# An order of issue written out for each engine, in place of a list scheduler with tables of offsets

## The chip, the cores and the metric

The kernel runs on one core of one Trainium2 chip. The metric is the device time of an execution in microseconds, as the median of several runs.

## The reference

Sequence S = 2048, model width D = 640, 32 heads of 20, hidden width F = 1728. All arrays are float32.

```python
def _A_ref(x, wqkv, wo):            # sliding, dilated attention
    W, dil = 8, 2
    q, k, v = split(x @ wqkv)       # 32 heads of 20
    idx = pos[:, None] - (jnp.arange(W) * dil)[None, :]
    logits = einsum("bhsd,bhswd->bhsw", q, k[idx]) * scale   # -1e9 where idx < 0
    o = einsum("bhsw,bhswd->bhsd", softmax(logits), v[idx])
    return o @ wo

def _B_ref(x, w1, b1, w2):          # dense, Mish, dense
    h = x @ w1 + b1
    return (h * jnp.tanh(softplus(h))) @ w2

x = A_x
g = sigmoid((x * gate_w).sum(-1, keepdims=True))
return g * _A_ref(x, wqkv, wo) + (1 - g) * _B_ref(x, w1, b1, w2)
```

## The kernel before

**The work.** Every float32 operand of a matmul is split into two halves: a "high" one that ScalarE (ACT) copies out of the loaded buffer, and a "low" one, the difference, which VectorE (DVE) or GpSimd (POOL) subtracts (`split`, L865 to L878: the ACT copy is L873, the subtraction L876). Each product is three matmuls on TensorE (PE): high x high, high x low, low x high (`mm3`, L932 to L934). A buffer of two halves is a `pair`, a landing buffer a `raw`, an `hb` or a `z`.

The stages, in the order of time: projections to q, k, v for eight units of work (two halves of the sequence by four groups of eight heads; `qkv`, with the first group written as passes at L1074); beside them the first dense layer in blocks, most of them as "quads" that need seven products in place of eight and use sums and differences of blocks (`quad`, `sum_into`, L1227); the attention of each unit on DVE in large operations of 128 x 2560 elements (L985 and L988 for the scores, L1023 and L1032 for the outputs); then the second dense layer (`mlp2`, matmul groups at L1687 and L1688), also with such sums; then the output projection (`wo_out`), with additions of PSUM banks to SBUF on DVE (L1919) and a gate multiplication (L1607). Attention outputs, activations and sums go through DRAM and come back. SyncE (SP) issues almost all DMAs; POOL issues the 52 that accumulate into DRAM (`plus`, L1170).

There are seven PSUM banks for matmuls. A projection's bank is emptied by small ACT copies (L1080, L1082, L1084, and L1086 for the gate's column in the first group of heads); a quad takes up to five banks.

**The order.** The program is written as 2668 tasks, numbered as they are made, each with an engine, a cost in ns, the tasks it waits for, and the buffers it takes and holds. 412 elementwise tasks are for "ANY" engine, which means DVE or POOL. `Plan.run` (L565) plays the tasks through in an event loop when the kernel is built, and issues each task's instructions at the moment its engine is idle and the task is ready. Among ready tasks it takes the least by rank and by due time on PE; both are shifted by five tables of offsets for single tasks (`MOVED`, `HELD_BACK`, `NEEDED`, `RANKED`, `ENGINE`, L81 to L525). A task for either engine goes to whichever asks for it first, within the rules of L619 to L631. On each engine, instructions run on the chip in the order in which they were issued, with semaphores between engines.

A large attention operation on DVE sets `quiet`, and a POOL task placed while it runs waits, by a semaphore, for the DVE instruction before it (`follow`, L656):

```python
                    if e == "POOL" and on and quiet > now and gate and ins:
                        self.follow(ins, gate)
```

The planner's costs: a DVE operation of n columns 75 + 1.03 n ns, times 1.025; a POOL operation 100 + 2.4 n; a large attention operation 2820, times 1.025; a DMA 450 to issue, its bytes at 330 B/ns on one wire, and 3000 more until it counts as landed.

Of the kernel before, what the change touches and what calls it, by code (L numbers as in the profile page):

```python
# [46 lines left out]
class Buf:  # L47
    def __init__(self, ring, make):
        self.ring, self.make, self.left, self.t, self.gone, self.can = ring, make, 0, None, None, None


class Ring:
    def __init__(self, n):
        self.free, self.line, self.at, self.left = n, [], 0, list(range(n))
# [12 lines left out]
class Task:  # L67
    def __init__(self, eng, ns, fn, rank, land):
        self.eng, self.ns, self.fn, self.rank, self.land = eng, ns, fn, rank, land
        self.waits, self.then, self.take, self.hold, self.both = 0, [], [], [], eng == "ANY"  # L70

def table(text):
    return {int(k): float(v) for k, v in (x.split(":") for x in text.split())}

MOVED = """2:-13 3:-34 5:27 6:38 7:-80 9:-9 10:16 12:-67 14:59 15:-7 17:-61 18:86 19:68 21:-84 22:-63 23:72 25:89 27:8 29:8  # L81
# [446 lines left out]
class Plan:  # L528


    NEAR, TURN, PATIENCE, HOP, STAY, HELD = 3564, 1936, 11000, 6531, 3456, 14750

    ORDERED = 1
    LAG = {"PE": 220, "ACT": 220, "DVE": 200, "POOL": 150, "SP": 3000}
# [30 lines left out]
    def run(self):  # L565
# [10 lines left out]
        for i, t in enumerate(self.tasks):  # L576
# [4 lines left out]
            if not t.waits:  # L581
                (shared if t.both else ready[t.eng]).append(t)
# [1502 lines left out]
```

## Time and profile before

| | |
|---|---|
| median of 3 runs | 617.6 us (616.7 to 618.37) |
| profiled execution | 616.73 us, its span 615.0 us |
| PE busy | 608.9 us (99%) |
| DVE busy | 577.1 us (94%) |
| ACT busy | 387.9 us (63%) |
| POOL busy | 311.2 us (51%) |

The span runs from the first to the last instruction of the profiled execution. Engines run side by side, so busy times do not add up. A matmul's end is modelled in the profile and lies beyond the start of the next one; the distance between starts tells its pace. In rows with a tile such as `pair<-raw`, the left name is written and the right ones are read; `side` and `bank` lie in PSUM, the others in SBUF. Behind `<-` in square brackets, or after "idle before", stands what ended the engine's idle time.

### The profile page before, as it was taken

The numbers are of one execution on the slowest core, as the hardware profiler recorded it, in microseconds if no ns is written. First come the engines' busy times: TensorE is split into PE (matmuls) and PEld (weight loads), VectorE is DVE, ScalarE is ACT, GpSimd is POOL, SyncE is SP. The second block draws the span as 40 slices with busy tenths as digits, with TensorE's granted clock in tenths as the row PEclk, the third lists the DMA queues.
The fourth block names the chain that finished last, engine by engine and source line by source line (L and its number), as shares of the span: only waits on it lengthen the run. The fifth ranks groups of instructions, "written<-read, shape, count | busy, mean of one in ns | idle before, by whom it ended". The sixth has DMA issues, their size and how long they took to land.

```text
span 615.0 us, 8940 instructions
## 1 busy us (share of the span) xinstructions
PE 608.9 (99%) x2693; PEld 504.7 (82%) x2693; DVE 577.1 (94%) x531; ACT 387.9 (63%) x854; POOL 311.2 (51%) x293
## 2 busy tenths in 40 slices
PE   8999999999999999999999999999999999999997
PEld 6888888888888888788888888888888888888885
DVE  4999999999998999999999999999999999999962
ACT  5746774768575767876666654583867574684721
POOL 2736566476283654654457657668554444601200
PEclk9999999999999999999999999999999999999999
DMA  8864679999999689999998999789999998996423
GB/s 301 254 192 149 178 220 305 280 252 305 257 268 300 172 240 273 261 242 259 291 267 219 286 289 290 243 245 299 332 377 352 283 386 276 321 354 197 147 89 119
DMA packets 106128, 159.43 MB, mean 259 GB/s; under 512 B 12112, under 2 KB 47952, under 8 KB 106048
## 3 DMA queue, kind: packets, MB, share of 16 engines
q1 hardware_dynamic: 98976, 146.01, 73.2%
q0 software_dynamic: 7104, 12.85, 13.7%
q8 instruction: 21, 0.34, 0.2%
q14 instruction: 27, 0.22, 0.1%
HBM read 91.90 MB, written 64.36 MB: 254 GB/s over the span
## 4 chain that ended last, share of the span: by engine, by line
PE 98%; DMA 1%; ACT 0%; SPq 0%; issue 0%; ACTq 0%
PE bank L932 32%; PE bank L934 32%; PE bank L933 32%; DMA z<-in_wq 1%; PE bank L1687 1%; PE bank L1688 1%; PE bank L1074 0%; SPq L882 0%; ACT pair L873 0%; ACT kvq L1801 0%; ACT kvq L1080 0%; ACT kvq L1082 0%; ACT hx L1084 0%; ACT zt L1086 0%; ACTq L1801 0%
## 5 line engine op out<-in xcount | busy, mean ns | idle before, releaser
L932 PE MATMUL bank<-pair,pair 128*128 128x512 f32 (+2 forms) x774 | 299.5, 387 | 0.4 <-ACT zt L1086 0.4
L933 PE MATMUL bank<-pair,pair 128*128 128x512 f32 (+2 forms) x774 | 299.7, 387 | 0.0
L934 PE MATMUL bank<-pair,pair 128*128 128x512 f32 (+2 forms) x774 | 299.7, 387 | 0.0
L932 PEld LDWEIGHTS bank<-pair,pair 128*128 128x128 f32 x774 | 145.4, 188 | 29.4 <-ACT zt L1086 0.8
L934 PEld LDWEIGHTS bank<-pair,pair 128*128 128x128 f32 x774 | 145.4, 188 | 28.7
L933 PEld LDWEIGHTS bank<-pair,pair 128*128 128x128 f32 x774 | 145.3, 188 | 28.7
L876 POOL TENSOR_TENSOR pair<-raw,pair 128x512 fp32r<-128x512 f32 (+3 forms) x82 | 104.8, 1303 | 86.9 <-ACT pair L873 30.2
L876 POOL TENSOR_TENSOR pair<-pair 128x512 fp32r<-128x512 f32 (+1 forms) x65 | 82.9, 1294 | 56.5 <-ACT pair L873 21.6
L873 ACT ACTIVATE pair<-pair 128x512 fp32r<-128x512 f32 (+1 forms) x139 | 79.6, 612 | 38.8 <-DMA pair<-act 18.7
L1023 DVE TENSOR_TENSOR pr<-kvq,side 128x2560 f32<-128x2560 f32 x32 | 90.3, 2822 | 1.1
L1032 DVE TENSOR_REDUCE kvq<-pr 128x320 f32<-128x2560 f32 x32 | 90.1, 2816 | 0.6
L988 DVE TENSOR_REDUCE lg<-pr 128x128 f32<-128x2560 f32 x32 | 90.0, 2812 | 0.6
L985 DVE TENSOR_TENSOR pr<-kvq,side 128x2560 f32<-128x2560 f32 x32 | 89.8, 2806 | 0.6 <-ACT lg L1000 0.5
L873 ACT ACTIVATE pair<-raw 128x512 fp32r<-128x512 f32 (+3 forms) x125 | 72.6, 613 | 18.5 <-PE bank L934 5.2
L1080 ACT ACTIVATE kvq<-bank 128x320 f32<-128x320 f32 x64 | 27.7, 434 | 49.1 <-PE bank L934 48.9
L876 DVE TENSOR_TENSOR pair<-pair 128x512 fp32r<-128x512 f32 (+1 forms) x74 | 46.7, 671 | 0.9 <-ACT pair L873 0.9
L932 PE MATMUL bank<-kvq,pair 128*128 128x512 f32 x102 | 40.0, 392 | 0.0
L933 PE MATMUL bank<-kvq,pair 128*128 128x512 f32 x102 | 39.8, 390 | 0.0
L934 PE MATMUL bank<-kvq,pair 128*128 128x512 f32 x102 | 39.8, 390 | 0.0
L1227 POOL TENSOR_TENSOR raw<-raw,raw 128x256 f32<-128x256 f32 (+1 forms) x25 | 24.4, 978 | 22.6 <-DVE side L1026 7.8
L876 DVE TENSOR_TENSOR pair<-raw,pair 128x512 fp32r<-128x512 f32 (+3 forms) x43 | 32.9, 785 | 1.7 <-ACT pair L873 1.7
L1374 ACT ACTIVATE bank<-bank 128x512 f32<-128x512 f32 x36 | 21.0, 584 | 13.7 <-PE bank L934 13.5
(119 smaller groups left out, 590.9 us busy)
## 6 DMA issues: line engine op xcount, KB each, us to landing
pair<-actt SPq DMA_DIRECT2D x54, 256.0 KB, 5.0
pair<-act SPq DMA_DIRECT2D x38, 256.0 KB, 4.8
raw<-in_w SPq DMA_DIRECT2D x34, 256.0 KB, 4.7
raw<-in_wq SPq DMA_DIRECT2D x30, 248.0 KB, 4.5
raw<-in_x SPq DMA_DIRECT2D x29, 256.0 KB, 5.1
actt<-hb SPq DMA_DIRECT2D x28, 256.0 KB, 3.6
actt<-z SPq DMA_DIRECT2D x24, 256.0 KB, 6.6
act<-z SPq DMA_DIRECT2D x24, 256.0 KB, 5.7
```

What stands on the lines that cost most here:

```text
L873: a = add("ACT", act_ns(n), lambda: A.activation(hi(), raw(), AF.Copy), after, rank=rank, take=take, hold=hold, kind="hi")
L876: return (V if e == "DVE" else G).tensor_tensor(lo(), raw(), hi().bitcast(F32), op=OP.subtract)
L932: nc.tensor.matmul(ps, ah, bh, start=first, stop=False, skip_group_check=more)
L933: nc.tensor.matmul(ps, ah, bl, start=False, stop=False, skip_group_check=more)
L934: nc.tensor.matmul(ps, al, bh, start=False, stop=last, skip_group_check=more)
L985: return V.tensor_tensor(pr, window(kv, s0, 0), qs[:, :, None, :].to_broadcast([128, 2, W, QF]), op=OP.mult)
L988: return V.tensor_reduce(lg_w[:, s0:s0 + 2], pr.rearrange("p s w (h d) -> p s w h d", d=DH), op=OP.add, axis=AX.X)
L1023: return V.tensor_tensor(twos, vw, pw[:, :, :, :, None, None].to_broadcast([128, 2, W, HQ, DH // 2, 2]), op=OP.mult)
L1032: return step("DVE", 2820, lambda: V.tensor_reduce(q[:, s0:s0 + 2].rearrange("p s (f j) -> p f s j", j=2), by_place, op=OP.add, axis=AX.X) ...
L1080: a = add("ACT", 330, lambda: A.activation(kv[:, 7 + s], ps.t[:, QF:3 * QF].rearrange("p (a b) -> p a b", a=2), AF.Copy), [done] + before, ...
L1227: return (V if e == "DVE" else G).tensor_tensor(t.t[:, i:i + n], a.t[:, j:j + n], b.t[:, k:k + n], op=op)
L1374: return add("ACT", 590, lambda: A.activation(to.t, of.t, AF.Copy), after, rank=-0.6, take=[to], hold=[of], kind=kind)
```

## The change

The five tables, the ranks, the due times and the event loop's choices are gone. In their place stands `ISSUE`, which lists for each of the five engines its tasks in the order of issue (and with that, for each "ANY" task, which engine does it), and `TAKEN`, which says for five rings of buffers which engine takes the next one. `Plan.run` walks the five lists: at each step it works out when the head of each list could start, and issues the earliest. Buffers go by the time at which they become free.

The planner's model of DVE and POOL differs. A DVE operation that reads two SBUF operands is marked `alone`; every "ANY" task is so marked. A POOL task from the "ANY" kind does not start while an `alone` operation runs on DVE, nor so that it would run into the next one, and an `alone` operation does not start while such a POOL task runs. Each such POOL task is tied by a semaphore to a DVE instruction: the one running when it is to start, or the one before that. The costs change: a large attention operation 2740 ns, no factor of 1.025 on DVE (nor 1.1 on ACT), a POOL operation 120 + 2.2 n.

The tasks themselves, what they compute, and the sizes of all buffers stay.

```diff
-                    if e == "POOL" and on and quiet > now and gate and ins:
-                        self.follow(ins, gate)
...
+ISSUE = {
+    "PE": """1 96-110 115 120 125 135 130 140 145 232 244 240 236 263 267 290 294 298 302 376 377 380 381 386 388 425 389 426 390 429 430
...
+    "ACT": """7 4 13 10 19 16 22 25 47 31 28 41 38 35 44 111 50 116-118 121 56 119 53 59 72 126 62 131 132 136 127 128 122 74 133 123 78
...
+1108 1082 1109 1104 1009 1101 1006 1018 1177 1113 1178 1003 1114 1184 1127 1110 1115 1012 1116 1111 1105 1106 1121 1186 1015
...
+    "DVE": """0 8 5 14 11 20 17 26 23 32 29 42 48 36 39 45 51 60 68 69 54 70 63 57 75 84 79 85-87 216 161 162 155 164 220 165 185 167 186
...
+    "POOL": """2 73 71 95 213 93 218 210 91 219 89 225 231 227 250 229 276 253 278 271 277 256 283 362 259 287 285 289 364 373 262 363 409
...
+2109 1706 2112 2115 2136 2139 2163 2036 2145 2179 2182 2176 2190 2169 2201 2422 2210 2198 2204 2193 2252 2207 2069 2240 2275
+2278 2255 2072 2300 2428 2419 2375 2345 2368 2400 2378 2480 2413 2455 2458 2617 2560 2464 2478 2610 2588 2569 2586 2604 2607
+2602 2572 2612 2615""",
+    "SP": """6 3 12 9 18 30 15 24 21 27 34 46 40 49 37 215 43 52 65 55 58 64 61 66 33 67 80-83 208 151 150 211 214 248 152 272 153 222
...
+            if t.eng == "POOL" and t.both:
+                if single:
+                    s = max(s, over["DVE"] - 80)
+                elif before and s < over["DVE"]:
+                    s = max(s, before.own + 100)
+                if ahead and ahead[0] < s + t.ns - 50 and ahead[1].alone:
+                    s = max(s, ahead[0] + ahead[1].ns)
+            if t.eng == "DVE" and t.alone:
+                s = max(s, beside - 50)
...
+            if e == "POOL" and t.both:
+                gate = before if s < over["DVE"] - 80 else last
+                if gate and gate.ins and ins:
+                    self.follow(ins, gate.ins)
...
-        return 100 + 2.4 * n
+        return 120 + 2.2 * n
...
-            asked[0] = step("DVE", 2820, mul, [c] + after, kind="qk")
-            return step("DVE", 2820, red, kind="qk sum")
+            asked[0] = step("DVE", 2740, mul, [c] + after, kind="qk")
+            return step("DVE", 2740, red, kind="qk sum")
```

More of the change, by code (lines that the diff above doesn't have):

```diff
@@ L47, with __init__ @@
 class Buf:
-    def __init__(self, ring, make):
-        self.ring, self.make, self.left, self.t, self.gone, self.can = ring, make, 0, None, None, None
+    def __init__(self, ring, make, n=None, seeded=False):
+        self.ring, self.make, self.n, self.seeded, self.left, self.t, self.ended = ring, make, n, seeded, 0, None, 0.0
 class Ring:
     def __init__(self, n):
-        self.free, self.line, self.at, self.left = n, [], 0, list(range(n))
+        self.free, self.at = [(0.0, i) for i in range(n)], 0
 class Late:
@@ L67 @@
 class Task:
[L68 to L81, printed above, removed]
[94 rows of a table removed]
-2649:-13 2650:-99 2651:-49 2653:-23 2655:15 2656:76 2657:55 2658:2 2660:-81 2661:-30 2663:-88 2664:-30 2665:-15"""
@@ L519, with __init__ @@
-2649:-1 2650:-2 2653:1 2654:-2 2656:1.5 2657:1.75 2658:-0.25 2659:-0.25 2660:0.25 2663:2 2665:0.75 2667:-2.25"""
-ENGINE = """60:2 63:1 84:2 276:2 283:2 409:2 412:1 478:2 480:2 529:2 612:1 720:1 738:2 843:2 855:1 861:1 864:1 883:2 886:2 888:1
[4 rows of a table removed]
-2484:1 2485:2 2533:1 2566:1 2578:1 2583:1 2585:1 2588:1 2604:2 2606:1 2607:2 2612:1 2614:1 2615:2 2617:2"""
+    def __init__(self, eng, ns, fn, after, land, kind, alone):
+        self.eng, self.ns, self.fn, self.after, self.land, self.kind = eng, ns, fn, after, land, kind
+        self.alone = alone or eng == "ANY"
+        self.take, self.hold, self.both, self.done = [], [], eng == "ANY", None
@@ L540, in __init__, with buf, add @@
         self.tasks = []
[L541 removed]
         self.follow = follow
[L544 to L551 removed]
+    def buf(self, ring, make, n=None, seeded=False):
+        return Buf(self.rings[ring], make, n, seeded)
+    def add(self, eng, ns, fn, after=(), take=(), hold=(), size=0, kind="", alone=False, **wish):
+        t = Task(eng, ns, fn, [p for p in after if p is not None], size / 330.0, kind, alone)
         if eng == "POOL" and type(ns) is not tuple:
             t.ns = (ns, ns)
[L554 to L557 removed]
         t.take = list(take)
@@ L565, in run @@
     def run(self):
-        ready = {e: [] for e in self.LAG}
-        busy = dict.fromkeys(self.LAG, False)
-        events, n, left, wire = [], 0, len(self.tasks), 0.0
-        quiet, gate, last, shared, begun = 0.0, None, None, [], False
-        LARGE, TOUCH = ("qk", "qk sum", "pv"), ("qk", "w", "pv")
-        inside = {"DVE": "", "ACT": ""}
-        touched = copied = None
-        moved, held, needed, ranked, engine = map(table, (MOVED, HELD_BACK, NEEDED, RANKED, ENGINE))
-        for i, t in enumerate(self.tasks):
-            t.key = (t.rank, i + moved.get(i, 0))
-            t.late += held.get(i, 0)
-            t.bias, t.only, t.turn = needed.get(i, 0), engine.get(i, 0), t.rank + ranked.get(i, 0)
-            t.rdy = 0.0
-            if not t.waits:
-                (shared if t.both else ready[t.eng]).append(t)
@@ L583, in run @@
-        now = begun_pe = 0.0
-        pos = 0.0
-        for t in self.tasks:
-            if t.eng == "PE":
-                t.pos = pos
-                pos += t.ns
-        for t in reversed(self.tasks):
-            t.need = min((x.pos if x.eng == "PE" else x.need - self.HOP for x in t.then
-                          if x.eng == "PE" or (x.both or x.kind == "hi") and x.need is not None), default=None)
-            if t.need is not None:
-                t.need -= t.early
-        def due(t):
-            if t.need is None:
-                return now - t.rdy > t.patience
-            ahead = sum(x.need is not None and x.need < t.need for x in shared)
-            return t.need - begun_pe < self.NEAR + self.TURN * ahead
@@ L601, in fits @@
-        def fits(t):
+        TOUCH = ("qk", "w", "pv")
+        lines = {}
+        for e, text in ISSUE.items():
+            line = lines[e] = []
+            for x in text.split():
+                a, _, b = x.partition("-")
+                line.extend(self.tasks[i] for i in range(int(a), int(b or a) + 1))
+            for t in line:
+                assert t.eng == e or t.both and e in ("DVE", "POOL")
+                t.eng = e
+                if type(t.ns) is tuple:
+                    t.ns = t.ns[e == "DVE"]
@@ new lines, in run, with places @@
+        assert len({id(t) for line in lines.values() for t in line}) == len(self.tasks) == sum(map(len, lines.values()))
+        at, left, free, wire = dict.fromkeys(lines, 0), len(self.tasks), dict.fromkeys(lines, 0.0), 0.0
+        over, kind = dict.fromkeys(lines, 0.0), dict.fromkeys(lines, "")
+        beside, single, before, last, touched, copied, whole = 0.0, False, None, None, None, None, set()
+        taken = {self.rings[k]: v for k, v in TAKEN.items()}
+        def places(b):
+            return [x for x in b.ring.free if not b.seeded or x[1] in whole]
@@ L602, in fits, with start @@
+        def start(t):
+            s = free[t.eng]
+            for p in t.after:
+                if p.done is None:
+                    return None
+                s = max(s, p.own if p.eng == t.eng and not p.land else p.done)
             want = {}
             for b in t.take:
-                want[b.ring] = want.get(b.ring, 0) + 1
-                if b.ring.free < want[b.ring] or b.ring.line[b.ring.at + want[b.ring] - 1] is not b:
-                    return False
-                if b.can and not b.can():
-                    return False
@@ L717, in run @@
-        return now
+                n = want[b.ring] = want.get(b.ring, 0) + 1
+                can = sorted(x[0] for x in places(b))
+                if len(can) < n or b.ring in taken and ENGINES[int(taken[b.ring][b.ring.at + n - 1])] != t.eng:
+                    return None
+                s = max(s, can[n - 1])
+            if t.eng == "POOL" and t.both:
[5 more added lines that the diff above has]
+                    s = max(s, ahead[0] + ahead[1].ns)
@@ new lines, in start @@
+            if t.eng == "DVE" and t.alone:
+                s = max(s, beside - 50)
+            if t.eng == "DVE" and t.kind in TOUCH and kind["ACT"] == "qs":
+                s = max(s, over["ACT"])
+            if t.kind == "qs" and kind["DVE"] in TOUCH:
+                s = max(s, over["DVE"])
+            return s
+        while left:
+            first, ahead = (None, None), None
+            for e in ENGINES:
+                if at[e] < len(lines[e]):
+                    t = lines[e][at[e]]
+                    s = start(t)
+                    if e == "DVE" and s is not None:
+                        ahead = s, t
+                    if s is not None and (first[1] is None or s < first[0]):
+                        first = s, t
+            s, t = first
+            if t is None:
+                raise RuntimeError(f"nothing can go on, {left} left")
+            e = t.eng
+            at[e] += 1
+            left -= 1
+            for b in t.take:
+                can = [x for x in places(b) if x[0] <= s]
+                x = min(can, key=lambda x: (b.n is not None and x[1] in whole, x[0]))
+                b.ring.free.remove(x)
+                b.ring.at += 1
+                b.slot = x[1]
+                if b.n:
+                    (whole.add if b.n == 512 else whole.discard)(b.slot)
+                b.t = b.make()
+            t.ins = ins = t.fn(e) if t.both else t.fn()
+            if e == "POOL" and t.both:
+                gate = before if s < over["DVE"] - 80 else last
+                if gate and gate.ins and ins:
+                    self.follow(ins, gate.ins)
+            if t.kind == "qs":
+                if touched:
+                    self.follow(ins, touched)
+                copied = ins
+            if e == "DVE" and t.kind in TOUCH:
+                if copied:
+                    self.follow(ins, copied)
+                touched, copied = ins, None
+            t.own = end = free[e] = s + t.ns
+            over[e], kind[e] = end, t.kind
+            if e == "DVE":
+                before, last, single = last, t, t.alone
+            if e == "POOL" and t.both:
+                beside = end
+            if t.land:
+                wire = max(wire, end) + t.land
+                end = wire + (0 if e == "SP" else self.ADDING if t.kind == "plus" else 4000)
+            t.done = end + self.LAG[e]
+            for b in t.hold:
+                b.left -= 1
+                b.ended = max(b.ended, t.done)
+                if not b.left:
+                    b.ring.free.append((b.ended, b.slot))
@@ L720 @@
+        return max(t.done for t in self.tasks)
 @with_exitstack
@@ L730 @@
     banks = [psum.tile([128, 512], F32, name=f"bank{i}") for i in range(NBANK)]
-    unused, whole = list(range(NBANK)), set()
     pe = ctx.enter_context(tc.tile_pool(name="pe", bufs=1, side="right"))
@@ L743, in ps_buf @@
     def ps_buf(n=512, seeded=False):
-        at = []
-        def make():
-            i = next(i for i in sorted(unused, key=lambda i: i in whole) if i in whole or not seeded)
-            unused.remove(i)
-            at.append(i)
-            (whole.add if n == 512 else whole.discard)(i)
-            return banks[i]
-        b = plan.buf("bank", make)
-        b.gone = lambda: unused.append(at[0])
-        if seeded:
-            b.can = lambda: any(i in whole for i in unused)
+        b = plan.buf("bank", lambda: banks[b.slot], n, seeded)
         return b
@@ L1550, in load_step @@
         loaded[i] = p, at, acts
-    places = list(range(11))
     def place():
-        at = []
-        def make():
-            at.append(places.pop(0))
-            return kvq[1][:, at[0] * 512:(at[0] + 1) * 512]
-        b = plan.buf("b", make)
-        b.gone = lambda: places.append(at[0])
+        b = plan.buf("b", lambda: kvq[1][:, b.slot * 512:(b.slot + 1) * 512])
         return b
```

196 lines of the change are left out of this document (50 added, 146 removed), and 494 rows, old and new, of tables (ENGINE, HELD_BACK, ISSUE, MOVED).

## The prediction

> **What bounds the kernel now.** I read the page first, then who TensorE (PE) waited for, then busy time by stage, then the order of time around each place where PE was late.
>
> ```profile
> span 615.0 us, 8940 instructions
> PE 608.9 (99%) x2693; PEld 504.7 (82%) x2693; DVE 577.1 (94%) x531; ACT 387.9 (63%) x854; POOL 311.2 (51%) x293
> PEclk9999999999999999999999999999999999999999
> PE 98%; DMA 1%; ACT 0%; SPq 0%; issue 0%; ACTq 0%
> ...
> PE bank L856 <- DVE lg L852: 1.2, 1, 1.2
> PE bank L932 <- ACT zt L1086: 0.4, 1, 0.4
> PE bank L1074 <- ACT pair L873: 0.4, 1, 0.4
> ...
> 12.00:245.00 233.00, 233.00 (x1039) 194.77 (x1038) 225.52 (x176) 157.28 (x370) 131.59 (x123) 1.00 0.86 245
> 260.00:435.00 175.00, 175.00 (x784) 146.93 (x783) 171.03 (x132) 109.69 (x251) 109.32 (x108) 1.00 0.96 268
> 534.00:545.00 11.00, 11.00 (x50) 9.10 (x49) 10.94 (x19) 6.79 (x12) 0.14 (x1) 1.00 1.06 349
> 545.00:575.00 30.00, 30.00 (x132) 24.57 (x131) 29.20 (x46) 19.33 (x37) 6.21 (x4) 1.00 0.74 249
> 575.00:605.00 30.00, 30.00 (x132) 24.37 (x132) 21.13 (x35) 11.58 (x21) 0.00 (x0) 1.00 0.27 100
> 611.10:615.00 3.90, 0.00 (x0) 0.00 (x0) 0.00 (x0) 0.52 (x1) 0.00 (x0) 1.00 0.18 67
> ```
>
> The stage rows give length, then busy time with instruction counts for PE, weight loads, VectorE (DVE), ScalarE (ACT) and GpSimd (POOL). PE is the whole chain, at full granted clock, and from 12 to 245 and from 260 to 435 us it is busy without a gap. Only three idle stretches before it are put down to a releaser: 1.2 us ahead of the first warm-up matmul and two of 0.4. DVE is nearly as full (577.1 of 615.0), so it can become late at once, but PE's own stream is the bound.
>
> The change leaves the matmuls alone: the same 401 PE tasks, in almost the same order. So the question is only how much PE waiting there is to remove and how much the new order adds. The first 1.2 us and the 3.9 us behind the last matmul (a copy and the last output's landing) stay: both kernels warm up first and end on the same matmuls of the last block.
>
> **Step 1, the first loads: -0.5 us.**
>
> ```profile
> 4.70 2.98 PE L1074 MATMUL bank<-pair,pair 128*128 128x498 f32 x12
> 8.06 2.98 PE L1074 MATMUL bank<-pair,pair 128*128 128x498 f32 x12 [0.37 <-ACT pair L873]
> 10.88 0.39 PE L932 MATMUL bank<-pair,pair 128*128 128x498 f32 x1
> ...
> 7.38 0.62 ACT L873 ACTIVATE pair<-z 128x498 fp32r<-128x498 f32 x1 [0.86 <-DMA z<-in_wq]
> ...
> 2.60 0.43 SPq L882 DMA_DIRECT2D bias<-in_b  x1
> 3.07 0.43 SPq L882 DMA_DIRECT2D z<-in_wq  x1
> ```
>
> Twelve matmuls take 10.88 - 8.06 = 2.82 us where nothing is late, but 8.06 - 4.70 = 3.36 us before them: 0.54 us lost. PE waited for ACT's copy of the second weight block, which waited for its load, the sixth that SyncE (SP) issued. The new list has this load (task 12) third and the bias (task 33) twenty-fifth. At 0.47 us an issue (3.07 - 2.60) three places are 1.4 us, more than the 0.54 lost, so the wait goes. Next in line is the third block of x, seventh in both lists; its ACT copy moves behind that of the third weight block, which can eat part. I take -0.5; bounds -0.54 and 0.
>
> **Step 2, the bank at 251 us: -0.6 us.**
>
> ```profile
> 250.42 0.39 PE L933 MATMUL bank<-pair,pair 128*128 128x498 f32 x1
> 250.65 0.38 PE L934 MATMUL bank<-pair,pair 128*128 128x498 f32 x1
> 251.46 0.50 PE L932 MATMUL bank<-pair,pair 128*128 128x512 f32 x1 [0.42 <-ACT zt L1086]
> ...
> 251.20 0.20 ACT L1086 ACTIVATE zt<-bank 128x1 f32<-128x1 f32 x1
> ```
>
> Matmuls start 0.23 us apart, here 0.81: 0.58 us lost. The first matmul of a quad (task 1175) waited for the last of four small ACT copies that empty a projection's bank (task 1111). In the new ACT list 1177, which copies what 1175 makes, stands ahead of 1111. So 1175 must start on a bank that does not need 1111, and this wait cannot come back. What is late next is the bank emptied by 1111, held longer; the quad's later banks could want it. I take -0.6; bounds -0.6 and 0.
>
> **Step 3, the small losses in the output stage: -0.15 us.**
>
> ```profile
> 581.84 0.45 PE L932 MATMUL bank<-kvq,pair 128*128 128x512 f32 x1
> 582.12 0.40 PE L933 MATMUL bank<-kvq,pair 128*128 128x512 f32 x1
> ...
> 586.75 0.49 PE L932 MATMUL bank<-kvq,pair 128*128 128x512 f32 x1
> 587.08 0.40 PE L933 MATMUL bank<-kvq,pair 128*128 128x512 f32 x1
> ```
>
> 0.28 and 0.33 between starts against 0.23 is 0.15 us, where PE takes halves that DVE has only just made. Doubled for gaps of a hundredth that I do not quote, 0.3 is the most to win; I take 0.15.
>
> **Step 4, work between DVE and POOL: hidden, but this sets the risk.** Counting the new lists against the engines in the trace, 57 elementwise tasks go from DVE to POOL (47 of about 512 columns, 1 of 384, 8 of 256, 1 of 128) and 40 come back (26, 2, 11, 1).
>
> ```profile
> L876 DVE TENSOR_TENSOR pair<-pair 128x512 fp32r<-128x512 f32 x65 | 42.7, 692 | 0.9 <-ACT pair L873 0.9
> L876 POOL TENSOR_TENSOR pair<-pair 128x512 fp32r<-128x512 f32 x59 | 76.9, 1322 | 41.0 <-ACT pair L873 18.5 <-DVE side L1026 6.9 <-PE bank L934 5.8
> L1447 POOL TENSOR_TENSOR raw<-raw,raw 128x256 f32<-128x256 f32 x17 | 12.5, 741 | 4.1 <-DVE side L1026 3.2 <-DVE pr L1023 0.3
> ...
> 567.59 4.70 POOL L1607 TENSOR_TENSOR kvq<-kvq,pair 128x512 f32<-128x512 f32 x3
> ...
> 568.32 1.11 DVE L1607 TENSOR_TENSOR kvq<-kvq,pair 128x512 f32<-128x512 f32 x1
> 569.36 1.78 DVE L1607 TENSOR_TENSOR hb<-hb,pair 128x512 f32<-128x512 f32 x1
> 571.06 0.68 DVE L1919 TENSOR_TENSOR kvq<-bank,kvq 128x512 f32<-128x512 f32 x1
> 571.66 1.78 DVE L876 TENSOR_TENSOR pair<-raw,pair 128x512 fp32r<-128x512 f32 x2
> ```
>
> An undisturbed 512-column DVE operation takes 0.60 us of its engine (571.66 - 571.06). Net, 21 large tasks leave DVE (12.6 us) and 1 of 384 and 3 of 256 come back (1.4 us by their columns): DVE 577.1 to about 566. POOL gets 21 x 1.32 less 1.0 (384 columns) and 3 x 0.74, some 24 us: 311 to 335 of 615. Neither becomes the bound by its sum. DVE's relief is worth nothing beyond steps 1 to 3, because PE has no other wait on it.
>
> The last rows show what the lists must avoid. Three POOL operations took 4.70 us; beside them DVE's with two SBUF inputs took 1.11 and 1.78 us instead of 0.68, while the one that reads a bank stayed at 0.68. So a POOL operation costs DVE between 0 (beside a reader of PSUM or a reduction) and 1.10 us (1.78 - 0.68), and saves it 0.60. [...]
>
> The new planner makes POOL wait for the running DVE operation of that kind and DVE for POOL, with 0.60 and 2.74 us, which fits the starts in the trace. It ties each shared POOL task to a DVE instruction by a semaphore; before, that was done only beside the large attention operations. Behind a waiting POOL task stand the rest of its list, the 52 accumulating DMAs that POOL issues among them, and PE waits for the halves. POOL's 304 us of idle time are the cover. If the plan slips, the price is the shift of one operation, 0.6 to 1.3 us, at each place where PE had no more to spare.
>
> **Step 5, the order of DMAs, of ACT and of the banks: +0.3 us.** SP keeps its 670 tasks in another order, as do ACT's 784. The count of Exp/Mish alternations in ACT's list falls from 29 to 27; at 1.28 us a table that is 2.6 us on an engine that is 63% busy.
>
> ```profile
> L1182 ACT ACT_TABLE_LOAD x14 | 18.0, 1283 | 2.0 <-issue 1.8
> pair<-actt SPq DMA_DIRECT2D x54, 256.0 KB, 5.0
> actt<-z SPq DMA_DIRECT2D x24, 256.0 KB, 6.6
> ```
>
> A load takes 5.0 us to land and a store before it 6.6; the planner counts 0.45 + 0.79 + 3.0 = 4.2 for 256 KB, in both kernels. An order fitted to that can leave PE waiting the difference, 0.8 to 2.4 us, wherever it cut a load fine. The lower end is no such place, the upper a few. The old order, planned with the same figure, has not one PE wait put down to a DMA, so I stay near the lower end: 0.3.
>
> **Sum.** 616.73 us (the profiled execution; 1.73 lie around its span) - 0.5 - 0.6 - 0.15 + 0.3 = 615.8. The median shown, 617.6, is 0.9 above that execution; what makes the others longer is not in this trace. I keep most of it (+0.7): **616.5 us**, 0.2% below 617.6. The least is 616.73 - 0.54 - 0.6 - 0.3 = 615.3; no edit touches PE's own 608.9 us, the start or the landing at the end.
>
> **The rivals.**
>
> *All waits go, and with them what made the other executions longer*: DVE has 11 us more room and PE runs through. That gives 615.3 for every execution, a gain of 2.3 us. For it speaks that both named waits are undone in the lists and that the planner's durations fit the starts; against it, that several PE starts late in the trace follow DVE's halves directly.
>
> *POOL takes DVE's time in the output stage* (slower). Behind 534 us there are no attention operations to run beside; DVE works on halves with two SBUF inputs and is busy 40.1 of 41 us until 575. There 16 tasks move to POOL, ten of them done before 575 in the trace. If each costs DVE 1.10 and saves 0.60, DVE is 10 x 0.5 = 5.0 us later at 575, and PE, which takes these halves at once, with it: 616.5 + 5.0 = 621.5. It decides, as a loss over 1.85 us, from 0.9 us a collision on (ten times 0.3 less the gains of 1.2). The three collisions shown added 4.70 us of POOL and about 0.43, 1.10 and 0.5 to DVE, 0.7 on average: near a wash. The bank additions on DVE (24, reading PSUM) offer places without a price. [...]
>
> *A load late in the new order of SP* (slower): two or three places at 0.8 to 2.4 us, about 4 us: 620.5. Against it: no such wait in the trace of before.
>
> *The order changes nothing that can be measured*: new waits of a microsecond replace the old, 617.6.
>
> **How the numbers follow.** About 0.3% (1.85 us) is what a measurement can tell from no change here: faster is below 615.75, slower above 619.45. My forecast with its neighbour "nothing changes" has 0.50 (0.47 within, 0.03 faster), all waits gone 0.30 (faster), POOL in the output stage 0.12 and a late load 0.08 (both slower). So faster 0.33, same 0.47, slower 0.20. The likeliest case alone spans 615.4 to 617.9. The range for 8 in 10 runs from 615.0, just under the least, to 620.8, which takes in a late load and half of the output-stage case.
>
> **What would show each step.** Step 1: no idle time before the thirteenth projection matmul near 7.7 us. Step 2: no PE wait on ACT's small copies near 251 us. Step 3: starts 0.23 us apart from 580 to 590. Step 4: POOL near 335 us, DVE near 566 or below, few DVE operations of 1.1 to 1.8 us; many of them behind 534 us with gaps in PE are the second rival. Step 5: a PE wait whose releaser is a DMA or the ACT copy of a loaded half. I am wrong if PE has idle time in its middle that adds up to over 3 us, or if its first real matmul starts later than 4.7 us.

## The result and the profile after

The changed kernel takes 625.4 us (median of 4 runs, 623.9 to 626.2), the kernel before beside it 618.0: a ratio of 1.0104, 95% interval 1.0070 to 1.0139. It is slower by 1%, and outside the range of 615.0 to 620.8. The profiled execution took 625.45 us. Of all runs below, one counts as slow, 632.4 us of m1_dve_margin, and is left out of that kernel's figures.

From the page of the changed kernel: span and busy time of each engine, then PE's busy share and its granted clock in 40 slices, then the chain by engine.

```profile
span 623.6 us, 8861 instructions
PE 612.6 (98%) x2693; PEld 506.5 (81%) x2693; DVE 565.7 (91%) x514; ACT 379.1 (61%) x852; POOL 331.4 (53%) x310
PE   9999999999999999999999999999799999999997
PEclk9999999999999999999999999999799999999999
PE 76%; DMA 8%; DVE 7%; issue 3%; SPq 3%; ACT 2%; POOL 1%; DVEq 0%; POOLq 0%; ACTq 0%
```

DVE and POOL moved as forecast (about 566 and 335). But PE, 98% of the chain before, is 76% of it now, and one slice in the middle shows a 7 in both busy share and clock. What PE waited for (us in total, times, the longest; the 1.2 ahead of the first warm-up matmul, as before, left out), then busy time by stage (the stage that holds the 7 stands by itself):

```profile
PE bank L509 <- DVE pair L452: 3.7, 1, 3.7
PE bank L508 <- ACT bank L950: 1.0, 2, 0.5
PE bank L509 <- POOL pair L452: 1.0, 1, 1.0
```

```profile
12.00:245.00 233.00, 232.45 (x1035) 194.14 (x1034) 218.38 (x184) 155.87 (x369) 120.86 (x113) 1.00 0.85 238
260.00:435.00 175.00, 173.59 (x772) 144.52 (x771) 167.07 (x131) 99.40 (x239) 106.54 (x107) 1.00 0.98 271
435.00:450.00 15.00, 11.21 (x38) 8.49 (x37) 13.91 (x15) 13.85 (x26) 6.99 (x6) 0.77 0.97 306
450.00:534.00 84.00, 84.00 (x373) 69.55 (x372) 77.41 (x74) 48.12 (x99) 57.49 (x48) 1.00 0.96 316
575.00:605.00 30.00, 30.00 (x133) 24.77 (x133) 25.12 (x38) 14.72 (x27) 11.51 (x10) 1.00 0.48 166
```

PE idles 0.55 us before 245, 1.41 from 260 to 435, and 3.79 in the 15 us behind, with the granted clock at 0.77 there. In the stages shown from 450 on it has no gap. The order of time on PE in that place (only starts count; the ends are modelled):

```profile
438.20 0.39 PE L510 MATMUL bank<-pair,pair 128*128 128x512 f32 x1
438.65 0.51 PE L508 MATMUL bank<-pair,pair 128*128 128x512 f32 x1
442.88 0.79 PE L509 MATMUL bank<-pair,pair 128*128 128x512 f32 x1 [3.73 <-DVE pair L452]
443.47 0.63 PE L510 MATMUL bank<-pair,pair 128*128 128x512 f32 x1
...
447.31 0.63 PE L510 MATMUL bank<-pair,pair 128*128 128x512 f32 x1
447.74 0.48 PE L508 MATMUL bank<-pair,pair 128*128 128x512 f32 x1
448.05 0.40 PE L509 MATMUL bank<-pair,pair 128*128 128x512 f32 x1
```

Starts are 0.23 us apart at full pace. From 438.65 to 442.88 there are 4.23 us, 4.0 too many: the second matmul of a group (task 1950) waits for a low half that DVE makes (task 1887). Behind it come 0.59 and then ten intervals of 0.427, about half pace: 0.36 and 10 x 0.20 = 2.0 more. One late half costs 6.4 us, over a third of it behind the wait. The granted clock in the trace is at half from 441.07 to 447.90 us, 6.83 us, and this is the 0.77.

Why the half was late is read from three engines, each ahead of the next in the chain.

```profile
433.25 0.84 DVE L516 STREAM_TRANSPOSE ot<-kvq 128x640 f32<-128x640 f32 x1 [1.70 <-DMA o<-ot]
434.02 0.38 DVE L585 TENSOR_TENSOR lg<-lg,mx 128x256 f32<-128x256 f32 x1
435.95 0.69 DVE L452 TENSOR_TENSOR pair<-pair 128x512 fp32r<-128x512 f32 x1 [1.55 <-issue]
436.56 2.81 DVE L561 TENSOR_TENSOR pr<-kvq,side 128x2560 f32<-128x2560 f32 x1
439.41 2.82 DVE L564 TENSOR_REDUCE lg<-pr 128x128 f32<-128x2560 f32 x1
442.14 1.28 DVE L452 TENSOR_TENSOR pair<-pair 128x512 fp32r<-128x512 f32 x2
...
426.91 1.16 ACT L449 ACTIVATE pair<-pair 128x512 fp32r<-128x512 f32 x2 [4.59 <-DMA pair<-s]
430.76 1.16 ACT L449 ACTIVATE pair<-pair 128x512 fp32r<-128x512 f32 x2 [2.18 <-DMA pair<-actt]
434.19 1.67 ACT L449 ACTIVATE pair<-pair 128x512 fp32r<-128x512 f32 x3 [2.27 <-DMA pair<-actt]
...
411.96 0.87 SPq L458 DMA_DIRECT2D kvq<-kvq  x1
...
420.09 0.94 SPq L458 DMA_DIRECT2D pair<-actt  x2
```

The half is the first of the two at 442.14, and stands in DVE's list behind two attention operations of 2.8 us. Those began late: DVE waited 1.70 for the output tile before to leave, and 1.55 more ahead of 435.95. The profile puts these 1.55 down to nothing ("issue"); I read them as a wait for a high half, because ACT's three copies from 434.19 on end at 435.86. They stand in ACT's list behind loads not landed yet (ACT idles 4.6, 2.2 and 2.3 us for loads). And SP issues without pause: twelve transfers from 411.96 to 420.09, 0.68 us each, where the planner counts 0.45.

### The profile page after: what moved, and what is told of

Its sections match the earlier page's. It is cut to its first block, busy times and chain, and to the rows that moved or that the text cites. A ratio compares the mean times of both kernels' runs of the same rounds, so it can differ in the third digit from the quotient of the medians.

```text
span 623.6 us, 8861 instructions
## 1 busy us (share of the span) xinstructions
PE 612.6 (98%) x2693; PEld 506.5 (81%) x2693; DVE 565.7 (91%) x514; ACT 379.1 (61%) x852; POOL 331.4 (53%) x310
## 4 chain that ended last, share of the span: by engine, by line
PE 76%; DMA 8%; DVE 7%; issue 3%; SPq 3%; ACT 2%; POOL 1%; DVEq 0%; POOLq 0%; ACTq 0%
PE bank L509 25%; PE bank L510 25%; PE bank L508 25%; SPq L458 2%; DVE lg L564 2%; DMA pair<-act 2%; DMA kvq<-kvq 2%; DVE pr L561 1%; DMA s<-raw 1%; DMA o<-ot 1%; POOL pair L452 1%; DMA pair<-actt 1%; PE bank L650 1%; DVE pr L599 1%; DMA pair<-s 1%
## 5 line engine op out<-in xcount | busy, mean ns | idle before, releaser
L452 POOL TENSOR_TENSOR pair<-raw,pair 128x512 fp32r<-128x512 f32 (+4 forms) x85 | 109.4, 1318 | 89.5 <-ACT pair L449 32.3
L452 POOL TENSOR_TENSOR pair<-pair 128x512 fp32r<-128x512 f32 (+2 forms) x81 | 101.8, 1280 | 68.3 <-ACT pair L449 22.4
L449 ACT ACTIVATE pair<-raw 128x512 fp32r<-128x512 f32 (+4 forms) x125 | 74.2, 618 | 28.9 <-DMA raw<-in_x 6.9
L452 DVE TENSOR_TENSOR pair<-raw,pair 128x512 fp32r<-128x512 f32 (+3 forms) x40 | 27.8, 711 | 6.8 <-ACT pair L449 6.8
L452 POOL TENSOR_TENSOR kvq<-raw,kvq 128x512 fp32r<-128x512 f32 x10 | 13.0, 1296 | 34.7 <-DVE pair L452 19.9
```

The costliest lines, as they stand in the source:

```text
L449: a = add("ACT", act_ns(n), lambda: A.activation(hi(), raw(), AF.Copy), after, rank=rank, take=take, hold=hold, kind="hi")
L452: return (V if e == "DVE" else G).tensor_tensor(lo(), raw(), hi().bitcast(F32), op=OP.subtract)
```

## The experiments

The theories, as they stood before the first run. T1: loads land late, as SP's queue is full and behind its plan. T2: the half that PE waits for stands at the wrong place of DVE's list. T3: the new ties, or operations of DVE and POOL running into each other, make the halves late. Later came T5: DVE's list has no time to spare, so PE has to wait for it in one place or another.

Ratios are to the kernel before, on the same chip; the versions ran on several chips, so a difference of 2 or 3 us between two of them is read from the ratios as well as from the medians. Task numbers are those of the lists. "Excess" is the distance between PE's starts over full pace, summed: 3.5 us in the kernel before, 12.1 in the changed one. One thing goes for every version that moves list entries: the planner runs again and places ties and buffers by its new starts. Of the changed kernel's 245 ties, 20 are gone or fall elsewhere in x1_low_first, 5 in x2_stores and 10 in x3_sp_relief, x8_loads_first and m2_both, and 35, 108 and 108 of 787 buffer places differ in the last three. So none of these five is the move alone.

**Does the order lose it, or what the change does around it?** The first two keep one and take away the other.

```diff
 k0_old_order: the kernel before's order of issue and of buffers, in the changed program
-ISSUE, TAKEN = (changed lists)
+ISSUE, TAKEN = (the order and engines that the kernel before's planner came to)
 x4_no_ties:
-                if gate and gate.ins and ins:
-                    self.follow(ins, gate.ins)
```

> The changed program with the kernel before's five lists of issue and its sequences of GpSimd's operations; the ties of GpSimd to VectorE and the tracking of tiles stay as changed. If the order itself loses the time (T1, T2: the lists have no margin), this runs like the kernel before, 617 to 619 us. If the ties, or GpSimd and VectorE locking each other out, lose it (T3), it stays above 622 us.

> The changed kernel without the ties that hold an operation of GpSimd back until a given one of VectorE has started (they order time alone, no data). T3 (the ties are what makes GpSimd or VectorE late): 4 us or more less, below 621 us. T1 and T2: the waits of TensorE at 438.65 us stay, within 1 us of the changed kernel, 624.5 to 626.5 us.

k0_old_order: 622.3 us, ratio 1.0078 (1.0054 to 1.0102). x4_no_ties: 661.0 us, 1.0708 (1.0642 to 1.0774). The first speaks for T3: the old order loses some 5 us too. The second speaks against the way in which I held it: without ties the kernel is 36 us slower, not faster. From the page of x4_no_ties, and from its waits:

```profile
PE 621.7 (95%) x2693; PEld 508.7 (78%) x2693; DVE 613.4 (94%) x514; ACT 379.0 (58%) x852; POOL 347.0 (53%) x310
```

```profile
PE bank L511 <- DVE pair L454: 12.3, 7, 5.2
PE bank L510 <- ACT bank L952: 8.4, 5, 5.6
```

The same DVE operations take 613.4 us in place of 565.7: 48 us more, as operations of DVE and POOL now run into each other, and PE waits for the halves. The theory that ties merely delay falls; the kernel lives on them, and which ones there are matters.

**Which ties does the old order lack?** The kernel before has 250 of them, each on a POOL task placed beside a large attention operation; the changed rule gives that order 229, 130 of them the same.

```diff
 k1_old_ties = k0_old_order, and
-                gate = before if s < over["DVE"] - 80 else last
+                the kernel before's 250 ties, task by task
 k2_plus_ties = k0_old_order, and 39 of those 250 beside its own
 k3_large_ties = k0_old_order without the 81 ties that stand beside no large operation
 k4_model_2820 = k0_old_order, where the model counts a large operation 2820 ns, not 2740 (51 of 229 ties and 78 of 787 buffer places differ)
```

> As k0_old_order (the kernel before's five lists in the changed program), and with the kernel before's own 250 ties of a GpSimd operation to a VectorE one, written out task by task, in place of the 229 that the changed model gives for that order (211 operations are tied in both, 130 of them to the same VectorE operation). If the ties, and not the order, lose the 5.3 us of k0_old_order, this runs like the kernel before, 616.5 to 618.5 us. If what loses them lies in the rest of the changed program (which buffer of a ring a tile gets, the order in which the instructions are written), it stays at 621 to 623 us.

> As k0_old_order with the changed model's own ties, and with 39 of the kernel before's ties beside them: those of the adding transfers that GpSimd issues (plus) and of two small loads, which the changed program no longer ties. If these are what k0_old_order lacks, 617 to 619 us; if it is the ties of the low halves and sums, 621 to 623 us.

> k0_old_order (the kernel before's lists in the changed program, 622.3 us) with only the 148 of its 229 ties that stand beside a large operation. If the 81 others are what it loses against k1_old_ties (618.0 us), 617.5 to 619.5 us; if what it lacks are ties that the kernel before has and the changed model doesn't give, 622 us or more.

> k0_old_order (the kernel before's lists in the changed program, 622.3 us) where the model that places the ties counts a large attention operation at 2820 ns, as the kernel before's did, and not at 2740 (2.81 us is measured). If the short count misplaces the ties, 618 to 620 us; if the rule does, 621 to 624 us.

| kernel | us | ratio (95%) |
|---|---|---|
| k1_old_ties | 618.0 | 1.0015 (0.9998 to 1.0031) |
| k2_plus_ties | 621.1 | 1.0075 (1.0047 to 1.0102) |
| k3_large_ties | 625.9 | 1.0128 (1.0081 to 1.0175) |
| k4_model_2820 | 619.9 | 1.0024 (1.0007 to 1.0041) |

With its own ties the old order runs like the kernel before, in the changed program. So the new placing of ties costs that order 4.3 us (622.3 - 618.0). The 39 ties of transfers are not it, and taking ties away does not help (625.9, with an interval that overlaps that of k0). More than half of the 4.3 goes when the model counts a large operation near the 2.81 that it measures, 2.4 us by the medians and 0.54 of 0.63% by the ratios. That with 2740 ns a POOL task is set beside the wrong operation is my reading, as k4 moves buffers too. The largest wait of PE in k0_old_order, which k4 does not have:

```profile
374.65 0.38 PE L508 MATMUL bank<-pair,pair 128*128 128x496 f32 x1
377.57 0.78 PE L506 MATMUL bank<-pair,pair 128*128 128x496 f32 x1 [2.54 <-ACT hx L658]
378.15 0.61 PE L507 MATMUL bank<-pair,pair 128*128 128x496 f32 x1
378.56 0.61 PE L508 MATMUL bank<-pair,pair 128*128 128x496 f32 x1
```

Ahead of it, the tied POOL sums at 347 to 352 us start up to 4.6 us later than in the kernel before, SP's loads behind them up to 5.5 us later, and ACT's copy that empties the bank stands behind one that waits 4.4 us for its load. Again the matmuls behind it run at about half pace, seven starts 0.41 us apart from 378.15 to 380.62, where 0.22 is the full pace of 496 columns.

**The same two edits in the changed lists.**

```diff
 x6_large_ties = changed kernel, and
-                gate = before if s < over["DVE"] - 80 else last
+                gate = before if s < over["DVE"] - 80 and kind["DVE"] in ("qk", "qk sum", "pv") else None
 x10_ties_2820 = changed lists and buffers; ties placed by the same rule with 2820 ns (38 of 246 differ)
```

> The changed kernel with 154 of its 245 ties of a GpSimd operation to a VectorE one: those of an operation that the model starts while one of VectorE's large attention operations runs, as the kernel before tied them. The 91 that it ties beside small operations, or behind an operation that by the model is over, go (they order time alone). If these 91 are what makes halves late on the chip (VectorE runs behind its plan and GpSimd is held back with it), TensorE's waits at 425 and 438 us go and it takes 616 to 620 us. If they keep GpSimd from running into VectorE's operations, more of VectorE's small operations take 0.5 to 1.1 us longer and it takes 626 us or more.

> The changed kernel's five lists and buffers as they are; the ties are placed anew by the same rule with a large attention operation counted at 2820 ns in place of 2740 (210 of 246 stay, 36 differ). In the kernel before's order the same step took 2.4 us off (622.3 to 619.9 us). If the short count misplaces ties in the changed order too, 2 to 3 us less: 622 to 623.5 us. If what it loses is in the lists themselves, 624.5 to 626 us.

x6_large_ties: 632.3 us, 1.0221 (1.0195 to 1.0247). x10_ties_2820: 631.1 us, 1.0210 (1.0164 to 1.0256). The better count, which helped the old order, makes the changed one 5.7 us worse, outside both of the values expected. That its lists were laid out for the ties that 2740 gives would explain it and is not shown. No set of ties tried makes the changed lists faster, so how much of their loss lies in ties was not settled.

**The late half itself, and what stands ahead of it.**

```diff
 x1_low_first, DVE:   ... 1879 1562 [+1887 1893] 1563 [-1887 1893] ...
 x2_stores, SP:       store 1344 behind 1346, stores 836 and 837 behind 835
 x3_sp_relief, SP:    1344 behind 1346; 1742, 1834 behind 1897; 1943 behind 1957; 1560, 2031 behind 2029
 m1_dve_margin:       pr.rearrange("p s w (h d) -> p s w h d", d=DH)[+ [:, :, :, :, 0:17]]
```

> The changed kernel with two small VectorE operations (the low halves of the pairs of tasks 1887 and 1893) moved ahead of one large attention operation of 2.8 us (task 1563). T2 (the half that TensorE waits for at 438.65 us stands behind two large operations in VectorE's list): the half is made at about 440 us instead of 443, TensorE's wait of 3.7 us falls to about 1 us, the 17 matmuls at 427 ns behind it are at 213 ns, and the time falls by about 6 us, to 619 us. T1 or T3 alone (VectorE is late whatever its order here): no change, 625 us.

(The intervals of 427 ns are ten, not 17, and at full clock matmuls of 512 columns start 227 ns apart in the trace, not 213.)

> The changed kernel with three stores of the output moved up on SP's queue (1344 to directly behind 1346; 836 and 837 to directly behind 835), so that the two transposes of VectorE at 317.4 and 433.25 us need not wait for the tile before to leave: VectorE's gaps of 2.27 and 1.70 us go. T1 (the last store holds up VectorE, and this makes the late half): TensorE's wait at 438.65 us falls by up to 1.7 us, and with it the slow matmuls, 2 to 4 us in all, 622 us. T2: the half stands behind ScalarE's late copy and two large operations all the same, less than 1 us, 624.5 to 625.5 us.

> The changed kernel with six transfers of SP's queue moved: four that nothing waits for until 435 us or later (tasks 1742, 1834, 1560, 2031: stores and loads, 2.6 us of SP's time between 402 and 420 us) and task 1943 behind the loads that ScalarE waits for at 427 to 434 us, and the store 1344 ahead to its three neighbours. T1 (loads land late because SP's queue is full from 381 to 437 us and 7 us behind its plan): the loads of tasks 1869, 1888 and 1897 are issued 2 to 2.5 us earlier, the halves at 438 us are made so much earlier, TensorE's wait of 3.7 to 4 us there falls to under 2 us and the slow matmuls behind it go; 620 to 622 us. If the loads are not what is late last (VectorE's own list, or ties): 624 to 626 us.

> The changed kernel, but the 32 sums over a head's twenty products (scores.red, 2.81 us each) take only seventeen of them, so that each is about 0.42 us shorter and VectorE has 13 us, 2.4%, less to do; the lists, ties and transfers are the same. If the loss comes of VectorE, which has no time to spare in the new lists and is 7 us behind its plan at 430 us, TensorE's waits at 425 and 438 us go and the time is 617 to 619.5 us. If it comes of loads that land late, for which ScalarE and with it the halves wait, VectorE's time does not matter: 623 to 625 us.

x1_low_first: 630.2 us, 1.0212 (1.0166 to 1.0257). x2_stores: 624.2, 1.0104 (1.0056 to 1.0152). x3_sp_relief: 625.1, 1.0130 (1.0106 to 1.0153). m1_dve_margin: 620.5 (nine runs, 619.2 to 628.0; 621.3 with the tenth), 1.0041 (1.0005 to 1.0077).

In x1 the excess at 439 us falls from 4.0 to 2.2 us, and one of 3.2 us appears at 460.6, where PE waits for a half from POOL; both are followed by slow matmuls (the mean granted clock of this execution is 0.994). T2 is right on the place; its price this run can't tell, as the planner's own count ends 5.4 us later with this move (620.8 against 615.5). In x2 DVE's two gaps are gone, and PE waits 2.9 us at 438.2 for another half, POOL's. x3 does what T1 said at 438 (no wait there, clock 1.000) and gains nothing. Its waits, without that of the warm-up:

```profile
PE bank L511 <- ACT bank L953: 2.0, 2, 1.6
PE bank L512 <- POOL pair L455: 1.7, 1, 1.7
PE bank L511 <- ACT hx L663: 1.3, 1, 1.3
PE bank L512 <- DVE pair L455: 0.9, 2, 0.7
PE bank L513 <- DVE pair L455: 0.6, 1, 0.6
```

In place of one wait of 3.7 there are several of up to 1.7: 176, 361, 428, and four between 460 and 500 us. The two at 176 and 361 lie ahead of every move, so no move made them (the changed kernel has the first, at 0.71 of excess, and not the second). They come of loads: ACT waits 3.15 and 3.14 us for transfers that it gets 9.7 and 6.6 us after SP issued them (the median of their kinds is 4.3 and 4.5 over the whole run). Those from 460 us on are for halves of DVE, which is still late. A lighter DVE gives some 4 us (a ratio of 1.0041 in place of 1.0104), but its runs spread: the five with a mean granted clock of 0.999 or 1.000 took 619.2 to 620.5, the four at 0.993 to 0.997 took 622.1 to 628.0. So half clock comes or stays away from run to run, and with it, as the one trace of them shows, a long pause (3.6 us of excess at 441.6 in the run of 628.0).

**All loads that were late, with and without a lighter DVE.**

```diff
 x8_loads_first, SP:  [+733] 642 [+730] 657 ... ; 1657 ahead of 1756, 1663 of 1634, 1776 of 1748, 1888 of 1885;
                      1344 behind 1346; 1742, 1834 behind 1897; 1943 behind 1957; 1560 behind 2029
 m2_both = x8_loads_first and m1_dve_margin
 x11_loads_2820 = x8_loads_first with ties placed by 2820 ns
```

> The changed kernel with eleven transfers of SP's queue moved: the loads that ScalarE waited longest for go ahead (tasks 733 and 730, which landed 8.5 to 9.5 us after issue at 174 to 176 us; 1657 at 359 to 362 us; 1663, 1776, 1888), stores and loads that nothing waits for go back (1742, 1834, 1943, 1560), and the store 1344 goes to its three neighbours. T1 (late loads alone make the loss): TensorE's waits at 176, 361 and 438 us go, and it takes 618 to 620.5 us. T5 (VectorE's list has no time to spare and runs late by itself; TensorE must wait for it once or in several places): the waits at 176 and 361 us go, 1 to 2 us, and what goes at 438 us comes back behind it, between 440 and 500 us; 623 to 625 us.

> x8_loads_first, and as in m1_dve_margin the 32 sums over a head's twenty products take only seventeen of them, so that VectorE has 13 us less to do. If late loads and VectorE's lack of spare time together make the whole loss, TensorE's waits behind 20 us come to under 2 us in all and it takes 616.5 to 618.5 us, against 621.3 us with the shorter sums alone. If the ties make a part that neither reaches, 619.5 to 621.5 us.

> Both repairs together, the moved transfers of x8_loads_first (622.3 us) and the ties placed with 2820 ns. If the two parts of the loss are separate and add up: 619 to 620.5 us. If the ties do not matter in the changed order, 622 us as x8_loads_first; if every repair only moves TensorE's wait to the next late half, 622 us or more too, with new waits between 400 and 500 us.

x8_loads_first: 622.3 us, 1.0063 (1.0041 to 1.0086), better than the changed kernel by 3.1 us of the medians and 0.41% (2.5 us) of the ratios, whose intervals overlap a little. m2_both: 622.8, 1.0066 (1.0045 to 1.0087). x11_loads_2820: 624.6, 1.0101 (1.0065 to 1.0138). ACT in x8_loads_first has no wait for the load at 173.2 us, and the waits that PE had at 176 and 438 in the changed kernel, and at 361 in x3, are gone. The longest that are left, in an execution of 624.8 us, the slowest of its six:

```profile
401.72 0.50 PE L511 MATMUL bank<-pair,pair 128*128 128x512 f32 x1
403.81 0.49 PE L512 MATMUL bank<-pair,pair 128*128 128x512 f32 x1 [1.59 <-DVE pair L455]
...
428.23 0.39 PE L511 MATMUL bank<-pair,pair 128*128 128x512 f32 x1
430.34 0.50 PE L512 MATMUL bank<-pair,pair 128*128 128x512 f32 x1 [1.72 <-POOL pair L455]
```

So late loads are a cause of the waits that go with them; that they are 3 us of the time is likely rather than shown, and they are not the whole. DVE's own time is not the rest: 13 us less of it (an estimate, 32 x 0.42) add nothing once the loads are moved (m2 missed both values expected), and POOL's half stays late, at 424.5 there. The other way round holds too: the moved loads add nothing to the lighter DVE, 622.8 against 620.5. T5 is half right: waits come back behind, but a lighter DVE does not cure them.

**Steps 1 and 2 alone.** The kernel before's program with its order, ties and buffers written out, and two edits taken from the changed lists:

```diff
 b1_replay_start
-SP 3 6 9 18 33 12 15 21 24 30 27 37 40 46      +SP 6 3 12 9 18 30 15 24 21 27 37 40 46 33
-ACT 4 7 10 13 16 19                            +ACT 7 4 13 10 19 16
-DVE 8 5 11 14 20 17 26 23                      +DVE 8 5 14 11 20 17 26 23
-ACT 1081 1082 1108 1109 1104 1105 1110 1106    +ACT 1104 1105 1106 1081 1082 1108 1109 1110
```

> The kernel before's program, its lists, ties and buffers written out, with two things of the changed kernel: the order of the first ten loads on SP with their copies on ScalarE and VectorE (the gap of 0.5 us at 7.3 us, step 1), and on ScalarE three small copies of a bank (tasks 1104 to 1106) ahead of task 1081 (the gap of 0.6 us at 250.65 us, step 2). Steps 1 and 2 of the prediction hold by themselves: both gaps go, nothing else moves, and it takes 1.0 to 1.3 us less than the kernel before, a ratio of 0.998. If any move in these lists is paid for elsewhere: ratio 1.000 or more.

617.1 us (12 runs), 618.0 before (28 runs): 0.9981 (0.9967 to 0.9994). It is the one version faster than the kernel before, by 0.9 us of the medians. A replay without the two edits was not run, so a share of the writing out itself is not excluded. PE's rows at both places:

```profile
4.81 5.03 PE L661 MATMUL bank<-pair,pair 128*128 128x498 f32 x21
...
250.65 0.39 PE L521 MATMUL bank<-pair,pair 128*128 128x498 f32 x1
250.88 0.39 PE L519 MATMUL bank<-pair,pair 128*128 128x512 f32 x1
```

The twenty-one first matmuls run on without the idle time that stood before the thirteenth, and the 0.81 us at 250.65 are 0.23. This one profiled execution shows two new pauses where nothing was touched (0.5 us at 71.4, 0.7 at 444.4), and its span, 615.2, is that of the kernel before; the gain, 0.9 us with an interval of 0.4 to 2.0, is that of the runs.

## Why the prediction was wrong

**Steps 1 to 3 held.** In the changed kernel the excess of the first 25 us falls by 0.52 (forecast 0.5), that at 251 us by 0.7 (0.6), that of 550 to 600 us by 0.29 (0.15). The 0.52 is net of a first real matmul at 4.82 us, later than the 4.7 that I had named as a sign of being wrong. b1_replay_start shows the first two by themselves.

**Step 4, the work moved, held as a sum:** DVE 565.7, POOL 331.4, and PE ran from 450 to 605 us without a gap in the stages shown, so the rival that put the loss in the output stage is wrong. Its collisions are there, as the mean of DVE's late halves shows (692 ns before, undisturbed 680):

```profile
L452 DVE TENSOR_TENSOR pair<-pair 128x512 fp32r<-128x512 f32 x51 | 41.5, 841 | 4.8 <-POOL pair L452 1.7 <-ACT pair L449 1.6 <-issue 1.5
```

What it got wrong is the tie, which I held to be hidden. I wrote that the new ties' price is "the shift of one operation, 0.6 to 1.3 us, at each place where PE had no more to spare". In the old order, where it could be measured, the changed ties cost 4.3 us, more than half of which went with a count of 2.82 us in place of 2.74 for operations that the profile shows at 2.81. I had both numbers and said that the planner's durations "fit the starts".

**Step 5 failed.** I set +0.3 us for the order of DMAs, ACT and banks, near the lower of two ends ("no such place" and "a few"), because the old order had not one PE wait put down to a DMA. That was evidence about the old order and none about the new one. Steps 4 and 5 together measured about +10 us, where I had 0 and +0.3: 12.1 - 3.5 = 8.6 in all, and 1.5 won by steps 1 to 3. Over six of them are the one place at 438 us. How much of the ten is the new ties and how much the order was not separated. Three terms were missing in step 5. The price of a late load does not stop at the difference in landing time: it went through ACT's, DVE's and POOL's lists to a half, 4.0 us in one place. With that pause of PE the clock was at half for 6.83 us, 2.4 us more. And I asked which waits go, not how early the halves are made. From the end of a subtraction to the first matmul that reads its half, behind 20 us, 23 of 289 halves in the kernel before had under 1.5 us, the nearest 0.63; in the changed one 23 of 290 as well, but three of these came late. So by this count the kernel before had no more to spare, and a shift of a microsecond or two could reach PE in either.

**The rival** "a load late in the new order of SP" had the start of the mechanism and 0.08 of the chance. Its 4 us were sized by the landing alone. My list of what would make me wrong named the right sign, idle time of PE over 3 us in its middle.

**What stays open.** Of the 7.4 us between the medians, the version with moved transfers has 3.1 less. In its one trace the waits left are for halves at 401 to 412, 428 and 475 to 500 us. Whether these come of ties or of the lists could not be told apart, as no set of ties tried suits the changed lists; the cause of this part stays open.

## What to carry to other kernels

An order fitted to a model pays on the chip for what the model has wrong. By the planner's own count the changed lists end at 615.5 us and the old ones, in the same program, at 618.7, which is 3.2 us better; the chip took 625.4 against 622.3. Before trusting such an order, ask of each stage how early the operands are ready, not only what waits today. When a wait goes at one place, look for it at the next before calling it won. Order and cross-engine ties belong together: a better count for the ties alone made the changed kernel 5.7 us slower.

## What the runs showed of the hardware that I had not expected

A long pause of PE cost more than itself. Over all profiled executions here, behind 20 us, the nine pauses of 3.1 us or more (excess, up to 5.8) were each followed by 5 to 11 matmuls at 0.41 to 0.43 us, 1.0 to 2.2 us in all; of six between 2.0 and 2.9 us three were (2.06, 2.22, 2.70) and three were not (2.26, 2.30, 2.81); none under 2.0 us was. Which ones can be read from the granted clock. In all eighteen traces it changes only at the edges of a grid of 3.41 us that starts where the clock first rises (in the changed kernel at 4.17, then 128 steps later at 441.07 and 130 at 447.90), and the idle time inside one step tells which steps were followed by half clock. Here are a step that holds the pause of 2.06 (x2_stores) with the next one, then three steps with the pause of 2.81, which lies across an edge (x4_no_ties); the clock is the third number from the end:

```profile
175.53:178.94 3.41, 1.51 (x7) 0.93 (x6) 3.37 (x3) 3.13 (x7) 1.42 (x2) 1.00 0.41 140
178.94:182.35 3.41, 3.41 (x10) 2.65 (x9) 3.41 (x4) 3.41 (x11) 3.31 (x3) 0.50 0.95 215
...
316.11:319.53 3.42, 2.42 (x11) 1.69 (x9) 3.39 (x2) 2.98 (x7) 2.51 (x3) 1.00 0.99 329
319.53:322.94 3.41, 1.76 (x8) 1.46 (x9) 3.41 (x3) 1.68 (x4) 2.68 (x3) 1.00 0.85 247
322.94:326.35 3.41, 3.41 (x17) 2.83 (x16) 3.38 (x3) 2.58 (x11) 2.55 (x3) 1.00 0.83 212
```

In excess, every full-clock step with 2.2 us or more inside it was followed by one or two steps at half clock, and none with 1.9 or less was.

What a tie is worth surprised me as well: 245 semaphore waits that carry no data save 36 us, because without them DVE needs 48 us more for the same 514 instructions. 64 of these are over 0.3 us longer there than the shortest of their kind, 68 us in all; with the ties 25 are, 20 us in all. Two of the 64 are 8.0 and 4.0 us longer. The longest, an operation of 0.38 us in the changed kernel, took as long as a row of POOL operations beside it:

```profile
502.49 8.33 DVE L587 TENSOR_TENSOR lg<-lg,mx 128x256 f32<-128x256 f32 x1
...
502.07 5.95 POOL L454 TENSOR_TENSOR pair<-pair 128x384 fp32r<-128x384 f32 x5
507.78 1.50 POOL L805 TENSOR_TENSOR raw<-raw,raw 128x512 f32<-128x512 f32 x1
509.02 1.50 POOL L454 TENSOR_TENSOR pair<-pair 128x512 fp32r<-128x512 f32 x1
```

The other 62 average 0.9, so my 0.7 for a collision was somewhat low. A POOL subtraction of 512 columns takes 1.43 us there (the mean of 73, 1.32 with the ties): the 62 cost less than that on average, and a row of POOL operations cost one DVE operation 8.0 us.
